# Parameter loads re-spaced, the tail's gap in another buffer, and more products in one pair: top-k attention with a low-rank mixer

## The chip, the cores and the metric

One core of one Trainium2 chip. The metric is the device time of the whole program in microseconds, the median of several executions. TensorE is called PE, VectorE DVE, ScalarE ACT, GpSimd POOL and SyncE SP.

## The reference

```python
# q, k, v: (8, 8, 576, 64);  top_k = 32
scores = q @ k.transpose(0, 1, 3, 2) / sqrt(64)
kth = np.partition(scores, -32, axis=-1)[..., -32:-31]
scores = np.where(scores >= kth, scores, -1e9)
attn = np.exp(scores - scores.max(-1, keepdims=True))
attn = attn / (attn.sum(-1, keepdims=True) + 1e-9)
x = (attn @ v).transpose(0, 2, 1, 3).reshape(8, 576, 512)
# U: (576, 32), V: (32, 576), w_ch1: (512, 2048), w_ch2: (2048, 512)
u = x + (x.transpose(0, 2, 1) @ U @ V).transpose(0, 2, 1)
out = u + np.maximum(u @ w_ch1, 0) @ w_ch2
```

The four mixer parameters arrive as 64-bit floats and are turned into 32-bit floats on the chip.

## The kernel before

**Work.** A "pair" is two heads of one batch; there are 32 pairs, four to a batch. The 576 query rows of a pair are cut into four tiles of 128 and a tail of 64. In the first batch each of the five tiles is a step of its own (steps n = 0 to 19, `ALONE` = 20). From the second batch on a pair has four steps, and the last of them holds tile 3 and the tail together, so step 23 is the first joint tail step. A step of the loop works on several tiles at once: scores for step n+1, the top-k search for step n, transposes, values and mixing for earlier steps.

**Top-k** runs on DVE: eight maxima at a time (L521, L539), which are then replaced by a large negative number (L534). In later pairs the row is first folded into an `upper` and a `lower` half: L395 copies the scores, L446 and L449 (POOL) and L448 (DVE) fold, L500 and L502 search the lower half. L448 of step n+1 stands inside the search of step n. `front` is a generator that writes this out in stages. For a tail in a joint step, the search works on a copy in a one-buffer tile `tplace` (slot 2 of the lanes).

**Gaps.** After the search, scores below the 32nd are pushed down: ACT forms a `gap` from the score and the threshold `least` (L565, L568), POOL subtracts it (L569), and ACT takes the exponential (L453). The gap lies in the tile `E`, a ring of two buffers. In a joint tail step there are three gaps.

**Queues.** Each engine runs its instructions in the order in which the loop writes them. On ACT the copy of a values product, `XT<-O` (L717), frees a buffer of the PSUM ring `tp` that the transposes (L631) need. From pair 6 on the transposes of whole tiles go by DVE (L595) and by DRAM (`away`, then `PT<-away`).

**Parameters.** They come in 36 parts: U in two, V in two, then 16 of `w_ch1` and 16 of `w_ch2`. `next_params(k)` makes one stage of a pipeline: it joins the parts whose passes are done, starts the passes of those that have been loaded, and issues k loads on SP. A part costs a load into `raw` (three buffers), three ACT passes (L179, L180, L183), one DVE shift (L202, or L193 for the last eight), and two POOL additions (L203, L205). The passes are put out one at each call of `fill`, the rest at the next `next_params`.

**Products.** The MLP of a batch is written as a generator that gives one matmul at a time: L842 for the first layer, L859 for the second, over 320 and then 256 rows. `fill`, called eight times a step, deals them out by a debt: each call adds `part` to `due`, and products are issued until `due` is paid. With no product left, `due` is set to 0. `part` is `share`, with a factor 1.4 in a joint tail step, and with a factor under 1 during the second batch:

```python
if n <= ALONE + BATCH + 2:
    part *= SECOND if ALONE + NT <= n < ALONE + 2 * NT else EARLY
```

The last batch's MLP (`closing`, L935) is computed after the attention in a Strassen-like form.

Of the kernel before, what the change touches and what calls it, by code (L numbers as in the profile page):

```python
# [8 lines left out]
F32 = mybir.dt.float32  # L9
# [17 lines left out]
def kernel(  # L27
# [29 lines left out]
    B, H, S, D = q.shape  # L57
    P = 128
# [4 lines left out]
    NT, TAIL = 4, 64  # L63
# [3 lines left out]
    NPAIR = H // 2  # L67
# [3 lines left out]
    ALONE = NPAIR * CH  # L71
# [11 lines left out]
    attn = ctx.enter_context(tc.tile_pool(name="attn", bufs=2))  # L83
# [63 lines left out]
    def f64_raw(srcs):  # L147


        n, w = srcs[0].shape[0], srcs[0].shape[-1]  # L150
        raw = mlpp.tile([P, 2 * C], U32, tag="raw", name="raw", bufs=3)
        if len(srcs[0].shape) == 3:
            raw = raw.rearrange("p (f w) -> p f w", w=w)
        else:
            raw = raw[:, 0:w]
        for i, src in enumerate(srcs):
            nc.sync.dma_start(raw[i * n : (i + 1) * n], src)
        return raw[0 : len(srcs) * n]

    def f64_parts(raw, out):  # L160

        n, w = raw.shape[0], raw.shape[-1] // 2
        d = "p f" if len(raw.shape) == 3 else "p"
        low, hi = (raw.rearrange(f"{d} (w two) -> {d} w two", two=2)[..., i] for i in range(2))
        low8 = raw.bitcast(U8).rearrange(f"{d} (w eight) -> {d} w eight", eight=8)[..., 3]
        if out is None:
            if not spare:  # L170

                uT = mlpp.tile([P, NC, S], F32, tag="uT", name="uT")
                words = uT.rearrange("p c n -> p (c n)").bitcast(U32)
                spare.extend(words[:, i * SLAB : (i + 1) * SLAB] for i in range(NT))
            out = spare.pop()[0:n, 0:w]
        bits = out.bitcast(U32)
        lows, his = low.bitcast(F32), hi.bitcast(F32)
        passes.extend((
            lambda: nc.scalar.activation(bits.bitcast(F32), his, AF.Copy, scale=RESCALE),  # L179
            lambda: nc.scalar.activation(  # L180
                lows, low8, AF.Identity, bias=four[0:n], scale=-(1 + 2.0**-10) * 2.0**-26
            ),
            lambda: nc.scalar.activation(his, his, AF.Sign, bias=nudge[0:n]),  # L183
        ))
        return hi, bits, low, len(params) < LATE

    def f64_join(hi, bits, low, late, outs):

        if late:
            none = nought if len(bits.shape) == 2 else nought.rearrange("p o -> p o ()")
            nc.vector.scalar_tensor_tensor(  # L193
                out=bits,
                in0=bits,
                scalar=3,
                in1=none.to_broadcast(list(bits.shape)),
                op0=ALU.logical_shift_left,
                op1=ALU.bitwise_or,
            )  # L200
        else:
            nc.vector.tensor_single_scalar(bits, bits, 3, ALU.logical_shift_left)  # L202
        nc.gpsimd.tensor_tensor(bits, bits, hi, ALU.add)  # L203
        for dst, form in outs:
            nc.gpsimd.tensor_tensor(dst.bitcast(U32), form(bits), form(low), ALU.add)  # L205
# [26 lines left out]
    def next_params(n):  # L232

        while passes:
            passes.pop(0)()
        while parts:
            f64_join(*parts.pop(0))
        while raws:
            r, outs = raws.pop(0)
            if isinstance(outs, list):  # L240
                parts.append((*f64_parts(r, None), outs))
                continue
            made = f64_parts(r, outs)
            parts.append((*made, [(made[1], same)]))
        for _ in range(min(n, len(params))):
            srcs, outs = params.pop()
            raws.append((f64_raw(srcs), outs))
# [6 lines left out]
    def load(g):  # L254

        list(loading(g))
# [177 lines left out]
    def split(g, t):  # L434

        if (g, t) in folds:
            pair(g, t, 1)

    def pair(g, t, stage):
        S2 = S2s[g, t]  # L440
        n = S2.shape[1]
        upper, lower = folds[g, t]
        top, bottom = upper[:, 0:n, 0:HALF], lower[:, 0:n].bitcast(U32)
        a, b = (ends_of(probs[g, t], i) for i in range(2))
        if stage == 0:
            nc.gpsimd.tensor_tensor(bottom, a.bitcast(U32), b.bitcast(U32), ALU.add)  # L446
        else:
            nc.vector.tensor_tensor(top, fronts_of.pop((g, t)), b, ALU.max)  # L448
            nc.gpsimd.tensor_tensor(bottom, bottom, top.bitcast(U32), ALU.subtract)  # L449
# [18 lines left out]
    def front(tiles):  # L468
# [5 lines left out]
        for g, t in tiles:  # L474
# [4 lines left out]
            n = S2.shape[1]  # L479
# [61 lines left out]
        for c, chunk, total, _, way in lanes:  # L541
            if way == "pooled":
                gap = attn.tile([P, S], F32, tag="E", name="E")
# [17 lines left out]
        if gaps:  # L561
            slots = [lane[0] for lane in gaps]
            lo, hi = min(slots), max(slots) + 1
            least = small.tile([P, 3], F32, tag="least", name="least", bufs=3)
            nc.scalar.mul(least[:, lo:hi], m8[:, lo:hi, 7], WIDEN)  # L565
            for c, chunk, *_ in gaps:
                gap = attn.tile([P, S], F32, tag="E", name="E")
                nc.scalar.activation(gap, chunk, AF.Relu, bias=least[:, c : c + 1], scale=-WIDEN)  # L568
                nc.gpsimd.tensor_tensor(chunk, chunk, gap, ALU.subtract)  # L569
            yield  # L570
# [586 lines left out]
    BATCH = NPAIR * NT  # L1157


    SLOTS, LONG, EARLY, SECOND = 8, 1.4, 0.91, 0.84  # L1160
    share = MLP_WORK / (NPAIR * SLOTS * (NT - 1 + LONG))
    fillers, mixing, due = [], [], 0.0

    def fill(k=1):


        nonlocal due
        for _ in range(k):
            if passes:
                passes.pop(0)()  # L1170
            if mixing and next(mixing[0], True):
                mixing.pop(0)
            part = share * (LONG if len(tiles(n)) > 1 else 1)
            if n <= ALONE + BATCH + 2:
                part *= SECOND if ALONE + NT <= n < ALONE + 2 * NT else EARLY
            due += part
            while due > 0:
                if not fillers:
                    due = 0.0
                    break  # L1180
                done = next(fillers[0], None)
                if done is None:
                    fillers.pop(0)
                elif not done:
                    due = 0.0
                else:
                    due -= done

    def tiles(n):

        return steps[n] if 0 <= n < STEPS else []
# [16 lines left out]
            yield from turns(g, t)  # L1208

    load(0)  # L1210
    next_params(3)
    t = 0
    for _ in prep(0):
        pass
# [3 lines left out]
    for n in range(STEPS + 2):  # L1218
        if n < STEPS:
            g, t = steps[n][0]  # L1220
            if t == 0 and g < NPAIR:
                load(g + 1)
            if t == (1 if g < NPAIR else 2) and g + 1 < NP:
                ready = prep(g + 1)
            fronts[n] = front(steps[n])
            next(fronts[n])
            if owed:
                inverse(owed.pop(), 0, 2 * NT + 1)
        else:
            t = NT  # L1230
        here, last = fronts.get(n, iter(())), fronts.pop(n - 1, iter(()))
        if n >= ALONE - 1 and n <= ALONE:
# [12 lines left out]
            if n < ALONE:  # L1245
                split(*steps[n + 1][0])
                next(here)
                next(here)
                inverse(g, 0, 2 * NT)
                mixing.append(mixed(g, 1))  # L1250
                fill()
                next(here)
                continue
            fill()
            scores(*steps[n + 1][0])
            fold(*steps[n + 1][0])
            next(here)
            while mixing:
                fill()
# [64 lines left out]
        if n < STEPS and n - 2 >= ALONE and len(tiles(n - 2)) > 1:  # L1324
            scale(steps[n - 2][0][0])
        next(here, None)
        if g == NPAIR and t < NT - 1:
            next_params(1)
        fill()
        if n >= STEPS:  # L1330
# [4 lines left out]
        next(here, None)  # L1335
        for tile_ in tiles(n + 1):
            split(*tile_)
        fill()
        next(here, None)
        for tile_ in tiles(n - 1):  # L1340
# [9 lines left out]
                coming = loading(g + 2) if g + 2 < NP else iter(())  # L1350
            next(coming, None)
        next(ready, None)
        if t != 0 or g == NPAIR + 1:
            next_params(1)
        next(here, None)
        fill()
# [36 lines left out]
```

## Time and profile before

| what | value |
|---|---|
| median of 3 runs | 1660.74 us (1660.58 to 1660.79) |
| profiled execution | 1660.23 us, its span 1658.0 us |
| mean granted PE clock | 0.968 |
| PE busy | 1555.6 us (94%) |
| DVE busy | 1546.9 us (93%) |
| ACT busy | 992.0 us (60%) |
| POOL busy | 1009.4 us (61%) |

Steps 0 to 19 end at about 202 us, the second batch's first pair (steps 20 to 23) at about 253 us, and the attention's last search at 1509 us. The PE records give a matmul as two records, one for each pass. A "gap" is idle time of an engine before an instruction, and the releaser is what ended it. Idle time of an engine off the critical path costs nothing by itself.

### The profile page before, as it was taken

What the parts mean: (1) busy time and instruction counts of PE and PEld (TensorE: products, weight loads), DVE (VectorE), ACT (ScalarE), POOL (GpSimd) and SP (SyncE); (2) the same over time, 40 slices, a digit from 0 to 9 for tenths busy, and PEclk for the clock granted to TensorE, in tenths of its full rate; (3) what the DMA queues carried; (4) which work ended last, traced back from release to release, by engine and by line L of the source; (5) the groups of instructions that cost most, each with busy time, mean ns of one, the idle gap of its engine ahead of it and who ended that gap; (6) DMA issues with size and microseconds to landing.
All of it is one profiled execution on the core that took longest, in us unless ns stands there. A gap on an engine that the chain in (4) does not pass through costs nothing.

```text
span 1658.0 us, 30248 instructions
## 1 busy us (share of the span) xinstructions
PE 1555.6 (94%) x9638; PEld 1182.7 (71%) x9638; DVE 1546.9 (93%) x4394; ACT 992.0 (60%) x2475; POOL 1009.4 (61%) x881
## 2 busy tenths in 40 slices
PE   4566698999999999999999999999999999999999
PEld 2344466787677877788777877788777877787776
DVE  7999998999999999999999999999999999994452
ACT  5888886665655566566655656565655656564320
POOL 4888756666656565656656565656666565653620
PEclk7787799999999999999999999999999999999999
DMA  4333321254445555454545455454545455543001
GB/s 113 98 101 99 86 76 25 57 133 135 126 130 137 133 154 133 131 139 130 134 125 141 128 154 133 134 137 131 133 126 141 128 151 134 136 123 109 7 2 28
DMA packets 280399, 189.42 MB, mean 114 GB/s; under 512 B 174288, under 2 KB 261168, under 8 KB 280240
## 3 DMA queue, kind: packets, MB, share of 16 engines
q1 hardware_dynamic: 259728, 117.62, 29.4%
q10 hardware_dynamic: 20512, 69.87, 13.1%
q8 instruction: 76, 1.25, 0.3%
q14 instruction: 83, 0.68, 0.1%
HBM read 116.49 MB, written 70.91 MB: 113 GB/s over the span
## 4 chain that ended last, share of the span: by engine, by line
PE 74%; DVE 19%; DMA 2%; POOL 1%; ACT 1%; issue 1%; SPq 1%; ACTq 0%; DVEq 0%; POOLq 0%
PE mm L859 23%; PE mm L842 22%; PE sc L350 7%; DVE m L539 7%; PE O L708 6%; DVE upper L534 6%; PE mm L935 3%; DVE first L521 2%; PE sc L382 2%; PE sc L935 2%; PE tp L935 2%; PE up L782 2%; PE O L705 1%; PE tp L631 1%; DMA PT<-away 1%
## 5 line engine op out<-in xcount | busy, mean ns | idle before, releaser
L842 PE MATMUL mm<-uT,w 128*128 128x320 f32 (+1 forms) x1792 | 463.3, 410 | 2.2 <-POOL uT L798 2.2
L859 PE MATMUL mm<-hT,w 128*128 128x320 f32 (+1 forms) x1792 | 460.2, 407 | 0.0
L569 POOL TENSOR_TENSOR Ssb<-Ssb,E 128x576 f32<-128x576 f32 x243 | 339.7, 1418 | 187.0 <-ACT E L568 187.0
L842 PEld LDWEIGHTS mm<-uT,w 128*128 128x128 f32 x1792 | 334.6, 191 | 102.0 <-issue 7.4
L859 PEld LDWEIGHTS mm<-hT,w 128*128 128x128 f32 x1792 | 332.0, 190 | 92.6 <-issue 10.2
L539 DVE MAX8 m<-upper 128x8 f32<-128x304 f32 (+1 forms) x774 | 362.3, 508 | 0.7
L534 DVE MATCH_REPLACE8 upper<-m,upper 128x304 f32<-128x304 f32 (+1 forms) x516 | 256.5, 504 | 0.0
L449 POOL TENSOR_TENSOR lower<-lower,upper 128x576 uint32<-128x576 uint32 x108 | 152.3, 1410 | 135.9 <-DVE upper L448 133.7
L446 POOL TENSOR_TENSOR lower<-Ssb 128x576 uint32<-128x576 uint32 x108 | 152.3, 1410 | 133.4 <-ACT Ssb L395 73.5
L453 ACT ACTIVATE Ssb<-Ssb,nmax 128x576 f32<-128x576 f32 x258 | 201.8, 784 | 15.7 <-POOL Ssb L545 7.8
L350 PE MATMUL sc<-qkT 64*128 64x288 f32 (+1 forms) x1056 | 177.2, 457 | 13.9 <-ACT Ssb L404 12.2
L568 ACT ACTIVATE E<-Ssb,least 128x576 f32<-128x576 f32 x243 | 176.2, 769 | 4.2
L502 DVE MAX8 upper<-lower 128x8 f32<-128x288 f32 x432 | 171.7, 438 | 2.7 <-POOL lower L449 2.7
L395 ACT COPY Ssb<-sc 128x576 f32<-128x576 f32 x216 | 127.6, 644 | 68.3 <-PE sc L350 68.1
L595 DVE STREAM_TRANSPOSE y<-Ssb 128x512 f32<-128x512 f32 (+1 forms) x312 | 154.0, 543 | 1.2 <-ACT Ssb L453 1.2
L708 PE MATMUL O<-PT,va 128*64 128x128 f32 x2048 | 143.7, 284 | 0.0
L854 ACT ACTIVATE hT<-mm 128x320 f32<-128x320 f32 (+1 forms) x224 | 91.2, 407 | 81.7 <-PE mm L842 78.7
L350 PEld LDWEIGHTS sc<-qkT 64*128 64x128 f32 (+1 forms) x1056 | 94.8, 195 | 54.7 <-issue 16.5
L708 PEld LDWEIGHTS O<-PT,va 128*64 128x64 f32 x2048 | 112.2, 139 | 16.2 <-issue 1.6
L534 DVE MATCH_REPLACE8 upper<-first,upper 128x304 f32<-128x304 f32 x216 | 97.4, 458 | 0.0
L500 DVE MATCH_REPLACE8 lower<-upper,lower 128x288 f32<-128x288 f32 x216 | 93.9, 442 | 0.0
L717 ACT COPY XT<-O 128x128 f32<-128x128 f32 x128 | 33.8, 264 | 98.3 <-PE O L708 94.0
(268 smaller groups left out, 2259.7 us busy)
## 6 DMA issues: line engine op xcount, KB each, us to landing
away<-y SPq DMA_DIRECT2D x416, 144.0 KB
PT<-away ACTq DMA_DIRECT2D x104, 576.0 KB
raw<-in_moe_w_ch_dram SPq DMA_DIRECT2D x32, 512.0 KB
va<-in_v_dram SPq DMA_DIRECT2D x64, 128.0 KB
scale<-rd ACTq DMA_DIRECT2D x56, 144.0 KB
out_dram<-ob SPq DMA_DIRECT2D x59, 128.0 KB
ld<-in_q_dram SPq DMA_DIRECT2D x108, 64.0 KB
ld<-in_k_dram SPq DMA_DIRECT2D x108, 64.0 KB
```

The costliest lines, as they stand in the source:

```text
L350: nc.tensor.matmul(out, lhsT=qkT[half(h), 0, cols(t)], rhs=qkT[half(h), 1, lo:hi], start=True, stop=True,)
L446: nc.gpsimd.tensor_tensor(bottom, a.bitcast(U32), b.bitcast(U32), ALU.add)
L453: nc.scalar.activation(E, chunk, AF.Exp, bias=nmax, scale=SCALE, accum_out=total)
L502: nc.vector.max(spot, lower)
L534: nc.vector.match_replace(nxt, ms[c], curs[c], NEG)
L539: nc.vector.max(ms[c], curs[c])
L568: nc.scalar.activation(gap, chunk, AF.Relu, bias=least[:, c : c + 1], scale=-WIDEN)
L569: nc.gpsimd.tensor_tensor(chunk, chunk, gap, ALU.subtract)
L595: nc.vector.transpose(y[:, :, i * NT : i * NT + c].rearrange("p r c j -> p c r j"), E2[:, a : a + c * P].rearrange("p (c r j) -> p c r j", ...
L708: nc.tensor.matmul(O[half(h)], lhsT=va[:, h, j, :], rhs=PT[:, NT * h + j], start=False, stop=(j == NT - 1),)
L842: nc.tensor.matmul(phs[f][:, 0:w], lhsT=first_layer(cc, f), rhs=uT[:, cc, lo:hi], start=(cc == 0), stop=(cc == NC - 1),)
L859: nc.tensor.matmul(po[:, 0:w], lhsT=w2[:, f, c * P : (c + 1) * P], rhs=hTs[f][:, 0:w], start=(f == 0), stop=(f == NF - 1),)
```

## The change

Four edits. The first `next_params` asks for two loads in place of three. The calls in the steps 21 to 23 are spread differently: three in step 21, three in step 22 and one in step 23, in place of two, two, one and one more in step 24. The tail's gap (slot 2) is written into `tplace` in place of `E`. The factor on `part` becomes one for each of the second batch's pairs: 1.1, 0.82, 0.91, 0.91, where it was 0.91, 0.84, 0.91, 0.91.

```diff
             for c, chunk, *_ in gaps:
-                gap = attn.tile([P, S], F32, tag="E", name="E")
+                if c == 2:
+                    gap = attn.tile([P, S], F32, tag="tplace", name="E", bufs=1)
+                else:
+                    gap = attn.tile([P, S], F32, tag="E", name="E")
                 nc.scalar.activation(gap, chunk, AF.Relu, bias=least[:, c : c + 1], scale=-WIDEN)
                 nc.gpsimd.tensor_tensor(chunk, chunk, gap, ALU.subtract)
...
-    SLOTS, LONG, EARLY, SECOND = 8, 1.4, 0.91, 0.84
+    SLOTS, LONG, EARLY = 8, 1.4, (1.1, 0.82, 0.91, 0.91)
...
             if n <= ALONE + BATCH + 2:
-                part *= SECOND if ALONE + NT <= n < ALONE + 2 * NT else EARLY
+                part *= EARLY[min(max(n - ALONE, 0) // NT, NT - 1)]
...
     load(0)
-    next_params(3)
+    next_params(2)
...
         next(here, None)
-        if g == NPAIR and t < NT - 1:
+        if g == NPAIR:
             next_params(1)
         fill()
...
         for tile_ in tiles(n + 1):
             split(*tile_)
+        if g == NPAIR and t < NT - 1:
+            next_params(1)
         fill()
...
         next(ready, None)
-        if t != 0 or g == NPAIR + 1:
+        if g == NPAIR and t < NT - 1:
             next_params(1)
         next(here, None)
```

## The prediction

> **What bounds the kernel now.** I read the page's busy lines and its 40 slices first, then a table of stretches of 20 us, then who waited for whom between 202 and 345 us, and last the order in time on three engines around the largest stall.
>
> ```profile
> span 1658.0 us, 30248 instructions
> PE 1555.6 (94%) x9638; PEld 1182.7 (71%) x9638; DVE 1546.9 (93%) x4394; ACT 992.0 (60%) x2475; POOL 1009.4 (61%) x881
> ...
> PE   4566698999999999999999999999999999999999
> ...
> DVE  7999998999999999999999999999999999994452
> ```
>
> Two engines are full, but not over the same time. DVE is full from slice 2 on and PE from slice 7 on; PE's share before that cannot be filled with MLP products, since these need the first batch's `uT`, and L842 first runs at 212.4 us.
>
> ```profile
> 240.00:260.00 20.00, 12.75 (x70) 9.04 (x69) 19.54 (x50) 9.36 (x22) 12.44 (x10) 0.89 0.11 17
> 260.00:280.00 20.00, 20.00 (x143) 14.99 (x143) 18.81 (x61) 14.24 (x37) 13.75 (x11) 0.94 0.16 40
> ...
> 640.00:660.00 20.00, 20.00 (x130) 14.71 (x126) 20.00 (x62) 13.27 (x34) 10.69 (x11) 1.00 0.54 143
> ```
>
> The columns are PE, PEld, DVE, ACT, POOL, granted PE clock, DMA share, GB/s. In 240 to 260 PE stands for 7.25 us and the clock is not full; from 260 on PE is dense and DVE is the one with holes; at 640 both are dense. DVE's gaps over 100 ns between 202 and 345 us add up to 7.3 us, and from there to 1495 us to under 0.5 us. So DVE paces 345 to 1500: a pair takes it 46.46 us every time (steps of 14.70, 11.40, 10.35, 10.01). At the end PE waits for the last probabilities again (1.37 us at 1517.8, 0.77 at 1528.0), so the tail hangs on DVE. What moves DVE at 330 us moves the end by as much.
>
> ```profile
> PE tp L631 <- ACT XT L717: 7.3, 1, 7.3
> ```
>
> ```profile
> DVE upper L448 <- ACT Stail L415: 3.4, 2, 2.5
> DVE upper L502 <- POOL lower L449: 1.9, 3, 1.0
> DVE y L595 <- ACT Ssb L453: 1.2, 2, 0.7
> DVE upper L448 <- ACT Ssb L395: 0.8, 1, 0.8
> ```
>
> One PE wait, and four kinds of DVE waits that sum to 7.3. The DVE waits come after it: PE is late with the scores because of it. Its cause, in order of time on ACT and then on POOL (start, length, instruction, and in brackets the idle time before it with its releaser):
>
> ```profile
> 252.65 0.21 ACT L565 ACTIVATE least<-m 128x3 f32<-128x3 f32 x1 [5.72 <-DVE m L539]
> 252.88 1.44 ACT L568 ACTIVATE E<-Ssb,least 128x576 f32<-128x576 f32 x2
> 257.32 0.78 ACT L568 ACTIVATE E<-Stail,least 128x576 f32<-128x576 f32 x1 [3.00 <-POOL Ssb L569]
> 258.00 0.74 ACT L183 ACTIVATE raw<-raw,nudge 128x512 f32<-128x512 f32 x1
> 258.65 0.42 ACT L854 ACTIVATE hT<-mm 128x320 f32<-128x320 f32 x1
> 258.96 0.26 ACT L717 COPY XT<-O 128x128 f32<-128x128 f32 x1
> ```
>
> ```profile
> 253.28 1.29 POOL L203 TENSOR_TENSOR w<-w,raw 128x512 uint32<-128x512 uint32 x1 [3.28 <-DVE w L193]
> 254.65 1.28 POOL L205 TENSOR_TENSOR w<-w,raw 128x512 uint32<-128x512 uint32 x1
> 255.88 2.77 POOL L569 TENSOR_TENSOR Ssb<-Ssb,E 128x576 f32<-128x576 f32 x2
> ```
>
> In step 23 the tail's gap is the third `E` of a ring of two. It waits for POOL's first subtraction, which stands behind a parameter's join. Behind the tail's gap on ACT stand a parameter pass, an `hT` and the `XT` copy that frees the buffer PE needs.
>
> **The change, part by part.** Step numbers are the loop's n; which instruction stands where is read from the two programs' order.
>
> *Parameters.* All 36 shifts (L202, L193) remain. Up to the start of step 20 there are 28 instead of 29: DVE and the MLP's start gain the 0.67 us of the L193 at 194.5. Steps 20 to 23 hold eight before the tail step's last maxima instead of five. The eight L193 rows run 0.64 to 1.44 us, mean 0.91; the long ones begin while a POOL subtraction or product runs and end about 0.55 us after it. Three more cost 2.7 us at the mean (1.9 to 4.3 at the ends). The last maxima, over at 252.61 before, end at 252.61 - 0.67 + 2.7 = 254.6. Given back behind them: the shifts at 252.54 (0.67) and 262.66 (1.16).
>
> On a page: the Trainium skill, "SBUF — State Buffer" ("two separate sides"), calls the port pair of VectorE and GpSimd "an exclusive lock, not a bandwidth split", the loser waiting for a whole instruction. This speaks against three joins in a step: if each of the three added shifts met the start of a subtraction of 1.4 us, they would cost 6.1 us, and the sum below would end near 0.8 us. The rows agree with the rule (1.33 and 1.44 us where POOL was busy, 0.64 to 0.67 where it was idle), but 0.70 us between two subtractions that follow each other shows that not every meeting costs a whole one.
>
> Queues passed: V's main load (four DMAs on SP) goes behind the second pair's eleven; these end at 17.7 us, so it lands by about 22 at the 126 GB/s of that stretch. ACT stands at its first pass ahead of step 0's `least`; before, it stood 8.7 us until 25.3 for V's tail at the same place, so nothing is later. In step 20 a second parameter load stands ahead of four `ld` issues on SP and holds them from 215 to about 222, until a join frees its buffer; L320 reads them at 235.5. POOL's join in step 23 now stands ahead of k=0's L449, but L449 waits for a fold on DVE that by my count ends some 2 us after the join. All this is costed at nothing; without that cover each would cost one join, 2.65 us.
>
> *The tail's row.* The gap in `tplace` waits only for DVE's last maximum on that row, which `least` needs anyway. In step 23 this and the moved join take 3.00 us of wait, the pass (0.65 net) and one `hT` (0.31) off ACT between 252.61 and the end of `XT` at 259.23: 6.62 becomes 2.66 us, and `XT` is done at 257.3. In the other 27 tail steps ACT's wait (26.2 us in all over 28) is worth nothing: DVE is dense there and does not read what ACT is late with.
>
> *Products.* A 128x320 product is two records of 0.27 us, 0.54 us of PE. In program order seven more are dealt by the values that run at 234.9 us before and ten by those at 247.8 (5.4 us); nine are still ahead at 288 (4.85), eight at 312 (4.3), eleven of the 256-wide ones (0.43 us each, 4.75) from 348 to 403, and none from 425 on. The batch's products only run out earlier, at 403 to 425 us, where PE waits for probabilities anyway (1.75 us at 403.1, 2.2 at 431.5). So the end has not one product less; what this part does is to fill the hole.
>
> PE reaches the transposes behind the hole at 252.03 - 0.67 + 5.39 - 0.54 (one product now stands after them) - 0.85 (two short gaps that close) = 255.4, and goes on at 257.3 with `XT` instead of 259.28: 2.0 us sooner, 0.54 of it returned by that one product. The granted clock was 0.50 from 255.5 to 262.3, in which PE worked 3.0 us; at full clock that is 1.5 us less. A gap of 1.75 us at 403 left the clock at 1.00, one of 2.2 us at 431 came with 0.91; the remaining 1.9 lies between, so this term is 0 or 1.5, and I take 1.5. By 323 us 1.2 us of products are paid back. Sum for PE at the scores of 326 us: 2.0 - 0.5 + 1.5 + 1.2 = 4.2 us sooner.
>
> The page "TensorE: Matmul & The Clock Gate" (Part 1) says that the clock halves after an idle window of about 3.4 us. By it 1.9 us would be safe and the sum 4.2; by the row of 2.2 us with its 0.91, which speaks against that rule, the sum would be 2.7.
>
> DVE: -0.67 + 2.7 - 0.67 - 1.16 = +0.2 at 263.7; then the waits for scores go, 0.80 and 2.52, giving -3.1. The 1.04 at 286.4 stays, since `oT` (0.87) now stands ahead of that L449 on POOL. The waits of 0.36, 0.67, 0.54 and 0.49 go, two of them because `oT` moves behind L449: -5.2, more than PE has, so the scores at 328.7 come with PE's -4.2. **Forecast: 4.2 us less.** The profiled execution took 1660.23 (span 1658.0 and 2.2 around it), 0.5 under the median of 1660.74; the difference goes on the median: 1656.5.
>
> **Rivals.**
> *The hole still halves the clock* (1.5 us lost), or the longer idle at 403 to 425 does it there. Each window of 3.4 us at half costs PE 1.7; behind 430 us its scores come as little as 0.4 us ahead of DVE. For: the 0.91. Against: PE gains about 1 us on DVE at 425. Either gives about 1658.0, within the 0.2%.
>
> *DVE pays more for its shifts.* At 1.44 us for each of the three, with the others dearer too, the maxima end at about 258 and the gain shrinks to 0.7: 1660.0. For: POOL has three joins of 2.65 and 2.8 us of subtractions in steps of 11 us. Against: it idled 3.3 to 3.6 us in each of these steps.
>
> *Slower: the ring of three raw buffers.* A load's turn is 4.0 us from issue to first pass at least (a row with no ACT wait), 2.15 of passes, 0.9 shift, 2.65 join: 9.7 us for three, against DVE steps of 11 to 12 us. If the landing took 10 us, a turn would be 15.7, DVE would stand some 4 us in both steps and end about 8 later: 1664.5. It decides from a landing of about 6 us; no row shows one.
>
> *The edits do nothing here* (every gain met by another wait in 260 to 330): 1660.7.
>
> **How the numbers follow.** A measurement tells 0.2%, 3.3 us, from no change. Forecast 0.55 (below 1657.4); clock or dearer shifts 0.29 and no effect 0.08 give 0.37 for the same; the ring 0.08. Lower bound: all 7.3 us of DVE's waits gone, 1653.4, so 1653.5; upper: dear shifts, 1660.0.
>
> **What would show it.** Right: no PE gap over 2.5 us near 255 us and a granted clock of 1.00 up to 280; ACT's tail gap without a wait; DVE's gaps in 255 to 345 under 3.5 us; eight L193 in steps 20 to 23 of 7 to 8 us; MLP products gone some 5 us earlier near 420. Wrong: ACT waiting at L179, DVE waiting at L193, or DVE's end moving by less than its step at 330.

## Result and the profile after

The changed kernel takes 1663.53 us (median of 22 runs, 1660.35 to 1665.85) against 1660.47 (22 runs, 1659.14 to 1661.83) of the kernel before: ratio 1.0016 with a 95% interval of 1.0009 to 1.0022, 3.1 us the other way from the forecast of 4.2 us less. A second set of 11 runs gave 1662.04 and 1.0011 (1.0002 to 1.0019). The profiled execution took 1661.79, with a span of 1659.6; it lies 1.7 us under the median, so the lines from it show about half of the loss. The changed kernel has three more lines above the tail's gap: what was L568 is L571 there, L631 is L634, L717 is L720, L842 is L845 and L854 is L857.

First, who waited for whom on the vector engine between 202 and 345 us (us in total, times, longest):

```profile
DVE w L193 <- ACT w L179: 3.2, 2, 1.7
DVE upper L502 <- POOL lower L449: 1.9, 1, 1.9
DVE upper L448 <- PE mm L862: 1.5, 1, 1.5
DVE upper L448 <- ACT Stail L415: 1.5, 1, 1.5
DVE y L598 <- ACT Ssb L453: 0.2, 1, 0.2
```

The lower four stand where the 7.3 us of before stood; 5.1 us are left there. The first is new and stands ahead of them: DVE waits at a parameter's shift for the first of that parameter's three passes on ACT.

PE in the same stretch, and the table of stretches (columns as in the prediction):

```profile
PE tp L634 <- ACT XT L720: 2.9, 1, 2.9
PE tp L639 <- ACT PT L635: 1.9, 1, 1.9
```

```profile
240.00:260.00 20.00, 17.99 (x108) 12.67 (x106) 20.00 (x42) 11.36 (x28) 11.81 (x10) 1.00 0.15 25
260.00:280.00 20.00, 18.98 (x117) 13.72 (x118) 19.96 (x69) 14.99 (x38) 14.79 (x11) 0.91 0.18 40
400.00:420.00 20.00, 16.76 (x129) 13.78 (x129) 19.97 (x65) 10.49 (x28) 13.17 (x11) 0.91 0.64 165
420.00:440.00 20.00, 16.53 (x91) 10.62 (x88) 20.00 (x60) 11.74 (x30) 11.54 (x12) 1.00 0.44 125
```

The hole of 7.25 us shrank to 2.93, but it ends at 260.92 us where it ended at 259.28, and the clock still loses a stretch of half speed behind it (0.91 of 20 us; the clock is 0.50 from 261.5 to 264.8 us, half as long as in the kernel before). The copy that PE waits for, in order of time on ACT:

```profile
258.38 0.21 ACT L565 ACTIVATE least<-m 128x3 f32<-128x3 f32 x1 [4.53 <-DVE m L539]
258.61 1.44 ACT L571 ACTIVATE E<-Ssb,least 128x576 f32<-128x576 f32 x2
259.96 0.76 ACT L571 ACTIVATE E<-Stail,least 128x576 f32<-128x576 f32 x1
260.63 0.24 ACT L720 COPY XT<-O 128x128 f32<-128x128 f32 x1
```

No wait stands between the subtraction's gap and the tail's any more, and from the last maxima to the end of `XT` it is 2.5 us instead of 6.6. But ACT starts at 258.38 instead of 252.65: DVE's last maxima end 5.7 us later. These 5.7 us more than undo the 4.1 us saved behind them. They add up as -0.7 of an earlier start, +3.2 of the two waits, and +3.25 of shifts (eight L193 sum to 8.03 us, five to 4.78).

Now the first wait on both engines. DVE and then ACT, in order of time:

```profile
219.25 1.40 DVE L539 MAX8 m<-upper 128x8 f32<-128x576 f32 x2
222.14 1.58 DVE L193 SCALAR_TENSOR_TENSOR w<-w,nought 128x512 uint32<-128x512 uint32 x1 [1.49 <-ACT w L179]
```

```profile
215.81 0.98 ACT L857 ACTIVATE hT<-mm 128x320 f32<-128x320 f32 x2 [1.48 <-PE mm L845]
...
220.13 0.44 ACT L857 ACTIVATE hT<-mm 128x320 f32<-128x320 f32 x1
220.58 0.78 ACT L453 ACTIVATE Ssb<-Ssb,nmax 128x576 f32<-128x576 f32 x1
221.26 0.18 ACT L453 ACTIVATION_READ_ACCUMULATOR Ssb<-Ssb,nmax 128x1 f32 x1
221.36 0.19 ACT L525 ACTIVATE nmax<-first 128x2 f32<-128x2 f32 x1
221.45 0.66 ACT L179 ACTIVATE w<-raw 128x512 f32<-128x512 f32 x1
```

ACT waits for nothing at L179: the raw words are there. The pass is simply late in ACT's own order, behind exponentials and evictions of products. A call to `next_params` deals the passes of the words that have come, and the next call deals their shift. In the kernel before, two rounds of maxima lie between these two calls, and the same pass and its shift, on ACT and on DVE, run without a wait:

```profile
221.61 0.66 ACT L179 ACTIVATE w<-raw 128x512 f32<-128x512 f32 x1
```

```profile
224.67 0.67 DVE L193 SCALAR_TENSOR_TENSOR w<-w,nought 128x512 uint32<-128x512 uint32 x1
```

The pass is no later in the changed kernel (221.45 us). With the third call only one round lies between, and it is DVE that comes earlier.

### The profile page after: what moved, and what is told of

Its sections match the earlier page's. It is cut to its first block, busy times and chain, and to the rows that moved or that the text cites. A ratio compares the mean times of both kernels' runs of the same rounds, so it can differ in the third digit from the quotient of the medians.

```text
span 1659.6 us, 30243 instructions
## 1 busy us (share of the span) xinstructions
PE 1557.6 (94%) x9638; PEld 1183.1 (71%) x9638; DVE 1547.6 (93%) x4394; ACT 991.8 (60%) x2475; POOL 1009.4 (61%) x881
## 4 chain that ended last, share of the span: by engine, by line
PE 72%; DVE 20%; DMA 3%; ACT 2%; issue 1%; SPq 1%; POOL 1%; DVEq 0%; ACTq 0%; POOLq 0%
PE mm L862 23%; PE mm L845 21%; PE sc L350 7%; DVE m L539 6%; PE O L711 6%; DVE upper L534 6%; PE mm L938 3%; DVE first L521 2%; PE tp L938 2%; PE sc L938 2%; PE sc L382 2%; PE up L785 2%; PE O L708 1%; DVE y L598 1%; PE tp L634 1%
## 5 line engine op out<-in xcount | busy, mean ns | idle before, releaser
L845 PE MATMUL mm<-uT,w 128*128 128x320 f32 (+1 forms) x1792 | 462.8, 409 | 2.6 <-POOL uT L801 2.3
L845 PEld LDWEIGHTS mm<-uT,w 128*128 128x128 f32 x1792 | 333.7, 190 | 104.3 <-issue 11.5
L539 DVE MAX8 m<-upper 128x8 f32<-128x304 f32 (+1 forms) x774 | 362.3, 508 | 0.7
L571 ACT ACTIVATE E<-Ssb,least 128x576 f32<-128x576 f32 x243 | 176.2, 768 | 4.2
L857 ACT ACTIVATE hT<-mm 128x320 f32<-128x320 f32 (+1 forms) x224 | 91.5, 409 | 86.4 <-PE mm L845 81.9
L720 ACT COPY XT<-O 128x128 f32<-128x128 f32 x128 | 34.0, 266 | 114.8 <-PE O L711 110.1
```

The source lines that it names most:

```text
L539: nc.vector.max(ms[c], curs[c])
L845: nc.tensor.matmul(phs[f][:, 0:w], lhsT=first_layer(cc, f), rhs=uT[:, cc, lo:hi], start=(cc == 0), stop=(cc == NC - 1),)
```

## Experiments

Theory A: the calls amid two steps cost what the other two parts gain, by these waits. Rivals: the products cost (D), or the gains are met by other waits (B). All times are medians; the difference is taken to the kernel before of the same set of runs.

| kernel | parts | us | difference | last maxima end | `XT` done | hole of PE near 260 | DVE's scores (L448) at about 328 |
|---|---|---|---|---|---|---|---|
| before | none | 1660.47 | 0 | 252.61 | 259.23 | 7.25 | 328.7 |
| e1 | tail | 1657.67 | -3.40 | 252.66 | 256.17 | 4.14 | 326.0 |
| e2 | parameters | 1663.41 | +2.34 | 256.84 | 260.66 | 5.21 | 330.1 |
| e3 | products | 1659.96 | -1.11 | 251.76 | 258.06 | 2.20 | 327.6 |
| e4 | tail, parameters | 1663.10 | +2.53 | 257.25 | 260.10 | 4.23 | 329.8 |
| e5, e11 | tail, products | 1654.77, 1655.41 | -5.80, -5.96 | 253.84, 251.40 | 257.03, 254.59 | none | 325.6, 323.1 |
| e6 | parameters, products | 1665.07 | +4.50 | 258.62 | 262.12 | 3.92 | 331.6 |
| after, e7 | all | 1663.53, 1662.04 | +3.06, +0.97 | 258.34, 258.82 | 260.87, 261.35 | 2.93, 2.95 | 330.4, 332.1 |

The columns from the fifth on are of one profiled execution each, whose own time lies up to 2.4 us from the median of its row (e5 above it; e2, e4, e6 and after 1.6 to 2.1 below). e5 and e11 have five runs each.

**e1, the tail's row alone.** The first hunk of the change.

> The kernel before with the tail's gap in the tail's row, and nothing else of the change. Theory A (the change loses by two waits of the vector engine for a parameter's pass, 1.49 and 1.72 us, that the products and the third call make together; each part by itself does what it was costed at): ACT's tail gap starts at about 254.3 instead of 257.3 us, the transposed copy that frees PE's buffer ends at about 256.2 instead of 259.2, PE's hole of 7.25 us shrinks to about 4.2, the clock still halves, and the time falls by 2 to 3 us, to 1657.5 to 1658.7. Theory B (what the scores gain is met by other waits behind 260 us): 1660.5, within 0.5 us of before.

1657.67 us, ratio 0.998 (0.9971 to 0.9989): theory A, and B falls. ACT in order of time:

```profile
252.70 0.21 ACT L565 ACTIVATE least<-m 128x3 f32<-128x3 f32 x1 [5.72 <-DVE m L539]
252.94 1.44 ACT L571 ACTIVATE E<-Ssb,least 128x576 f32<-128x576 f32 x2
254.28 0.76 ACT L571 ACTIVATE E<-Stail,least 128x576 f32<-128x576 f32 x1
...
255.92 0.24 ACT L720 COPY XT<-O 128x128 f32<-128x128 f32 x1
```

The tail's gap starts at 254.28 and the copy ends at 256.17. The hole is 4.14 us, and DVE's scores come 2.7 us sooner.

**e2, the parameter calls alone.**

```
-    next_params(3)
+    next_params(2)
...
-        if g == NPAIR and t < NT - 1:
+        if g == NPAIR:
             next_params(1)
...
+        if g == NPAIR and t < NT - 1:
+            next_params(1)
...
-        if t != 0 or g == NPAIR + 1:
+        if g == NPAIR and t < NT - 1:
             next_params(1)
```

> The kernel before with the parameter calls of the change, and nothing else of it. Theory A: without the added products ACT is not held by evictions of products, so the vector engine stands under 1 us in all ahead of the eight L193; these cost the 2.7 us of three more; the join no longer stands ahead of step 23's subtraction, so the copy that frees PE's buffer ends within 1 us of the 259.2 of before; 1659.5 to 1661.5. Theory C (one fill between two calls is enough for the wait, products or not): waits of 1.5 us and more at two of the eight, the last maxima at about 258 us, PE's hole over 9 us, and 1663 or more.

1663.41, ratio 1.0015 (1.0006 to 1.0024). Theory A falls and C has the time right: the waits at L193 are 2.6 us without a single added product (1.70 at 222.0 and 0.90 at 235.0). The three calls are enough for the waits. C's sizes were too large: only one wait is over 1.5 us, the last maxima end at 256.8 instead of about 258, and the hole is 5.21 us, not over 9.

**e3, the products alone.**

```
-    SLOTS, LONG, EARLY, SECOND = 8, 1.4, 0.91, 0.84
+    SLOTS, LONG, EARLY = 8, 1.4, (1.1, 0.82, 0.91, 0.91)
```

> The kernel before with the change's dealing of products, and nothing else of it. Theory A: PE's hole of 7.25 us near 255 is filled down to about 2 us and the clock does not halve there, or only after it; no wait at L193, since the shift stands two fills behind its pass; nothing is gained but the clock's 1.5 us: 1659 to 1660.7. Theory D (the products are what costs: ACT waits for them, and later holes of over 2 us near 415 and 432 us halve the clock): 1662 or more, with a granted clock of about 0.9 in 400 to 440.

1659.96, ratio 0.9991 (0.9982 to 1.0). The hole is 2.20 us and the mean clock in 240 to 260 us 0.96 instead of 0.89; behind the hole it is still 0.50, but from 258.2 to 261.6 us only. No wait at L193. Theory A, and D falls as the main cause. The gain of 1.1 us is not clear of the noise: the interval reaches 1.0, and the runs spread over 5.5 us (1657.06 to 1662.59).

**e7, the changed kernel again.**

> The changed kernel itself, once more beside the others. Median 1663 to 1664, with runs spread from 1660.4 to 1665.9 as before. If the spread comes of a few microseconds of idle PE that halve the clock in one run and not in another, a profile of over 1663 has more stretches with a granted clock under 1.00 than the one of 1661.8, and the same order of instructions; if it comes of landings of transfers, it has other waits for a DMA.

1662.04, under the median that was expected, spread 1660.76 to 1666.35. Its profile was of a run of 1663.68, 1.9 us over the first. Of that, 0.5 us is there at the last maxima (the two waits at L193 are 4.2 us here, and the first shift is 0.8 us shorter). The other 1.2 are there when DVE gets the scores after the hole (285.6 us instead of 283.9); the granted clock in 260 to 280 us is 0.83 instead of 0.91, one more stretch of half speed. No DVE wait for a DMA is behind it. So a half-clock stretch goes with most of what parts these two runs; that such stretches make the whole spread was not shown.

**e5 and e11, tail's row and products, without the parameter calls** (two sets of runs of one kernel).

> The kernel before with the tail's row and the products, without the parameter calls. Theory A (the parameter calls are what costs): no wait at L193; the copy that frees PE's buffer ends at about 256.2 us and PE reaches it at about 256.9, so the hole is under 1 us and the clock stays full there; the time is at or under that of the tail's row alone, 1655 to 1657.7. Theory D (the added products cost, by holes of over 2 us from 400 to 435 us that halve the clock, and they do so in some runs and not in others): median 1658 to 1660.5 with a spread of 4 us or more, against the 2 us of the tail's row alone.

> The tail's row and the products once more, beside the others: 1654.5 to 1655.5, the fastest of all, 5.5 to 6.5 us under before. Its first profile was of its slowest run (1657.14 us), with a clock of 0.66 in 180 to 202 us; if the early clock is what parts its runs, a profile of a run near 1654.8 has a higher clock there and ends its last maxima 1 to 2 us sooner, at 252 to 253 us, with the same order behind.

1654.77 and 1655.41, ratios 0.9968 (0.9955 to 0.998) and 0.9963 (0.9951 to 0.9976): the fastest of all, under both kernels of the change. All that is left of DVE's waits in e11, and the stretch where the hole was:

```profile
DVE upper L448 <- ACT Stail L415: 1.5, 1, 1.5
DVE upper L502 <- POOL lower L449: 1.0, 1, 1.0
DVE y L598 <- ACT Ssb L453: 0.2, 1, 0.2
```

```profile
240.00:260.00 20.00, 20.00 (x106) 14.29 (x103) 20.00 (x52) 15.50 (x36) 12.46 (x10) 1.00 0.09 14
260.00:280.00 20.00, 19.90 (x151) 14.82 (x150) 19.96 (x64) 14.20 (x37) 16.19 (x15) 1.00 0.17 40
```

PE and DVE are both full from 240 to 260 us at full clock: what the prediction wanted from the three parts, two of them do. e5's profile was of its slowest run, with a clock of 0.66 in 180 to 202 us; e11's had 0.84 there and ended its last maxima 2.4 us sooner, a little more than expected. One expectation failed: e5's profile has a wait of 0.8 us at L193, at 224.74 us, without the parameter calls. e11's has none, so DVE can come to that shift a little ahead of ACT's pass in the old spacing too; the calls make it two waits of 2.3 to 4.4 us in all.

**e4 and e6, the parameter calls with one other part.**

> The kernel before with the tail's row and the parameter calls, without the products. Theory A: the two waits at L193 are those of the parameter calls alone, 2.5 to 2.8 us, the hole of PE near 260 us is about 4 to 5 us, and the time is the tail's 1657.7 and the 2.3 us of the calls together, 1659.5 to 1661. Theory E (the calls already undo what the tail's row gains, since the vector engine and not the gap is then what the copy waits for): 1661.5 to 1663.5, no better than the calls alone.

> The kernel before with the parameter calls and the products, without the tail's row. Theory A: two waits at L193 of 3 us or more in all, since two products' evictions that wait for PE now stand ahead of the pass on ACT in step 20; the tail's gap waits about 1.4 us for a subtraction again; PE's hole near 260 us is 4 to 5 us; 1663 to 1665, above the change with all three parts. Theory D (products alone decide): within 1 us of the change.

e4: 1663.10, ratio 1.0014 (1.0005 to 1.0023), theory E: with the calls, the tail's row gains nothing over e2. The subtraction that the tail's gap waited for is no longer behind a join there, so there is only about 1 us to save (3.8 us from maxima to `XT` in e2, 2.85 in e4). e6: 1665.07, ratio 1.0026 (1.0016 to 1.0035), theory A, with 4.4 us of waits at L193: two products' evictions stand ahead of the pass and wait for PE, as in the lines of after at 215.81. So the parts are not a sum. The calls cost 2.3 us alone, 5.9 over the tail's row, 6.8 to 9.0 over tail's row and products.

**e8, the change with the passes dealt earlier.** The passes of the words that have come are dealt ahead of the step's exponentials; shifts and joins stay. Its lines behind the edit are four further on than in the changed kernel (L539 is L543, L571 is L575). The edit, shortened and with remarks added:

```
+        if g == NPAIR and t < NT - 1:
+            parted()              # the loop over raws, out of next_params
         fill()
...
-            next_params(1)
+            next_params(1, 1 if t < NT - 1 else 0)   # joins all but one
```

> The changed kernel, with the three passes of a parameter dealt one call earlier in steps 20 to 22 of the loop, ahead of the step's exponentials on ACT; the joins, shifts and loads stay at their places and every other engine keeps its order. Theory A (the vector engine's waits at L193 are waits for L179, which stands on ACT behind two exponentials and an eviction of a product): L179 ends at about 220 and 234.5 us, the two waits (3.2 to 4.2 us) are under 0.4 us in all, the tail step's last maxima end about 3 us sooner, at 255, and the time falls by 2 to 3.5 us against the changed kernel, to 1659 to 1660.5. Theory C2 (something else holds the vector engine there, the load of the raw words or the join on POOL): the waits stay at 3 us with another releaser, and the time stays within 1 us of the changed kernel's.

1660.41, ratio to before 1.0 (0.9991 to 1.0009): 0.2 us under its own before, where the change was 1.0 and 3.1 over. No wait at L193 is left; yet the last maxima end at 258.08, as late as ever. That was not expected of either theory. DVE, then POOL, in order of time:

```profile
219.56 1.40 DVE L543 MAX8 m<-upper 128x8 f32<-128x576 f32 x2
220.89 1.79 DVE L193 SCALAR_TENSOR_TENSOR w<-w,nought 128x512 uint32<-128x512 uint32 x1
...
225.38 1.63 DVE L193 SCALAR_TENSOR_TENSOR w<-w,nought 128x512 uint32<-128x512 uint32 x1
```

```profile
218.08 2.79 POOL L576 TENSOR_TENSOR Ssb<-Ssb,E 128x576 f32<-128x576 f32 x2 [3.36 <-ACT E L575]
220.82 1.30 POOL L203 TENSOR_TENSOR w<-w,raw 128x512 uint32<-128x512 uint32 x1
222.20 1.62 POOL L205 TENSOR_TENSOR w<-w,raw 128x512 uint32<-128x512 uint32 x1
...
225.16 1.29 POOL L205 TENSOR_TENSOR w<-w,raw 128x512 uint32<-128x512 uint32 x1
```

The shift that no longer waits starts while POOL adds, and ends 0.55 us after POOL's instruction: 1.79 and 1.63 us, where 0.67 would do. Three of the eight begin inside an addition of a join like that (1.79, 1.63 and 1.73 us) and three more inside another instruction of POOL, and the eight sum to 10.82 us. The wait did not go away; it moved into the shift. What e8 gains it gains behind the maxima: PE's hole there is 0.43 us, and the clock in 260 to 280 us is 1.00.

**e9, two loads at first instead of three, over tail's row and products.** It was meant to give the load saved to the end of step 20 as well, but that step is written out on a branch of its own which the edited line does not reach: the trace has five shifts before the last maxima as before, and one more at 271.6 us. So it tests the change's "two at once at first" alone.

```
-    next_params(3)
+    next_params(2)
...
-        if t != 0 or g == NPAIR + 1:
+        if g in (NPAIR, NPAIR + 1):
             next_params(1)
```

> The tail's row and the products, with two loads instead of three at once at first, and the load so saved given to the end of step 20, so that no step of 20 to 22 has more than two joins. Theory F (it is the third join in a step that costs: the shift meets ACT's late pass or a busy POOL there; what the second pays is the 0.7 us of the rows): the last maxima end 0.67 us sooner by the start and 0.7 to 1.5 later by the added shift, within 1 us of the tail's row and products alone, 1654 to 1655.8, and no wait at L193 over 1 us. Theory G (each join dealt into steps 20 to 22 costs 1.9 us, whichever it is, as the 5.7 us of three did): 1656 to 1657.5.

1655.94, ratio 0.9968 (0.9956 to 0.998), 5.4 us under before: within 0.5 us of tail's row and products. The start costs and gains nothing beyond that, so the loss of the change is the calls in steps 21 to 23, of which three each stand in 21 and 22. Neither F nor G was tried.

**e10, e8 with four joins left out on POOL**, those of the first and second calls in steps 21 and 22. The calls that choose them are not shown.

```
             nc.vector.tensor_single_scalar(bits, bits, 3, ALU.logical_shift_left)
+        if not join:
+            return
         nc.gpsimd.tensor_tensor(bits, bits, hi, ALU.add)
```

> The kernel with the passes dealt early, with POOL's two additions left out of four joins, those of the first and second calls of the first two steps after 214 us, so that these parameters come out wrong; DVE's eight shifts, ACT's passes and the loads stay. Theory H (with the waits gone, the shifts run 1.53 to 1.79 us each because POOL works at the same time: the price of a third join is paid on the vector engine as a wait or as a longer shift): the shifts that begin after a subtraction fall to about 0.7 us, the one at 231 that begins inside one stays at 1.4 to 1.6, the eight sum to 7.5 to 8.5 us instead of 10.8, the last maxima end at 255 to 256 instead of 258.1, and the time falls by 1 to 3 us, to 1657.5 to 1659.5. Theory I (the shifts are long for what they read and write, not for POOL): the eight still sum to over 10 us and the time stays at 1660 to 1661.

1657.25, ratio 0.9976 (0.9968 to 0.9985), theory H, a little beyond its ranges. DVE in order of time:

```profile
220.33 1.02 DVE L193 SCALAR_TENSOR_TENSOR w<-w,nought 128x512 uint32<-128x512 uint32 x1 [0.62 <-ACT w L179]
...
224.44 0.69 DVE L193 SCALAR_TENSOR_TENSOR w<-w,nought 128x512 uint32<-128x512 uint32 x1 [0.31 <-ACT w L179]
```

The two shifts of 1.79 and 1.63 us run 1.02 and 0.69 (the first still meets the end of a subtraction), and the third that met an addition runs 0.67 instead of 1.73; the one that begins inside a subtraction still runs 1.24. The eight sum to 7.24 us instead of 10.82. Of these 3.6 us, 2.8 are the three that met an addition; 0.8 is the first shift, at 206 us, ahead of the joins that are left out. Waits for L179 of 0.9 us come back, since DVE is early again. The last maxima end at 255.10, `XT` at 257.63, and 3.2 us of time go (4.0 when each is taken against the kernel before of its own set). The instruction on DVE is the same; what changed is how long POOL is busy beside it.

## Why the prediction was wrong

**The step that failed** is the costing at nothing of what the parameter calls move: "All this is costed at nothing; without that cover each would cost one join". It followed the calls past SP's queue and POOL's, and past ACT's at step 0 alone. In steps 21 and 22 it did not ask where on ACT the pass stands that the shift reads. It named the sign (DVE waiting at L193) but priced it only as a slow landing, which "decides from a landing of about 6 us". The landing was short: in the change a load issued at 223.20 us let its pass start at 226.95, 3.75 us later, and that was the one pass that waited for a transfer, 1.0 us, with no DVE wait behind it. The wait came from the distance of two calls, 3.2 us that no term held. The ring rival's 1664.5 us is the figure of the prediction that is nearest to 1663.53, but by luck: its landing of 10 us did not come.

**The shifts' term** was mis-sized as well, a little: three more at the "mean 0.91" are 2.7 us, and they took 3.25 in this profile and 2.5 in e7's (7.30 us for the eight), where the waits are 4.2. The two errors put the last maxima at 258.3 instead of 254.6 us. The rival of dearer shifts had that place right ("about 258"), by the other of the two causes, and e8 shows that they replace each other. But it let 0.7 us of gain stand, and by its own figures none could: 258 and the 2.66 us from there put `XT` at 260.7, 1.4 us later than before.

**On the port**, the prediction counted against the rule a row that fits it. The Trainium skill, "SBUF — State Buffer" ("two separate sides"), describes the ports that VectorE and GpSimd share as a lock that one of them holds for a whole instruction, for VectorE when it reads two inputs from SBUF and GpSimd reads there too. The prediction set its 6.1 us for three whole meetings aside for one row of 0.70 us. But that shift began at 229.36 us, 0.15 us before the first of two subtractions on POOL ended, and ended 0.55 us after it; the second subtraction, which began inside the shift, ran 1.87 us instead of 1.41. In all thirteen profiles every L193 that begins inside an instruction of POOL ends 0.54 to 0.55 us after that one, so a meeting costs what is left of it. For the change itself the mean of the rows was the nearer figure even so: 3.25 and 2.5 us against 2.7. Only in e8, without the waits, the eight shifts cost 10.82 - 4.78 = 6.0 us more than the five of before, and that this is near 6.1 is partly luck, since the meetings were not those that the 6.1 counted. In the change waits and shifts together cost 6.5.

**The tail's row** was right: 6.62 us "becomes 2.66", measured 2.5 in the change and 3.5 alone. Alone it is worth 3.4 us.

**The products** were right in kind: they filled the hole (7.25 to 2.20 alone, none with the tail's row), at a gain of 1.1 us alone (not clear of the noise) and 2.4 to 2.6 with the tail's row. But PE was to reach the transposes at 255.4 us and reached them at 258.0: 1.89 us of it is a new hole at 233 us, where PE waits for ACT's copies to `PT`. It goes with the calls: every kernel that has them shows it (1.75 to 2.57 us, and 0.30 in e10 without the joins), the others do not.

**The clock.** The hole was to be 1.9 us and was 2.93, and the clock halved. The rule of about 3.4 us on the page "TensorE: Matmul & The Clock Gate" (Part 1) would have kept it full there; it did not hold in these rows. Nor does the prediction's own reading, by which the clock halves from some length between 1.75 and 2.2 us on, hold in all runs (last section).

**The end** was right: the time follows DVE's step at about 328 us. Time less that start is 1331.3 to 1331.7 us in eleven of the thirteen profiled executions (1332.8 in e8, 1333.5 in e3). With the parameter calls left out the reasoning comes out near e5 and e11, which took 1654.8 and 1655.4: an estimate with e1's `XT` at 256.17, 3.1 us sooner than before, gives 3.1 - 0.5 + 1.5 + 1.2 = 5.3 us less in place of 4.2, or 1655.4.

## What to carry to other kernels

When a change deals work closer together, ask for each instruction that is moved up on the full engine where its producer stands in the producer's own order, not only whether its data has landed: the pipeline over three engines had a smallest distance between its calls here. Taking such a wait away gains nothing on that engine if the instruction then starts inside another engine's and pays the same time in its own length: price the wait and the meeting together. Here undoing the placement gained more than undoing the wait. Parts of a change are not a sum: two that gain 3.4 and 1.1 us one by one gain 5.9 together, and the third, which costs 2.3 alone, costs 6.8 to 9.0 on top of them.

## What the hardware showed that was not expected

- A shift of 0.67 us on DVE ran up to 1.79 us beside POOL's additions, and POOL's addition that began inside it ran 1.62 instead of 1.29 (e8, lines above): both sides pay, and the shift ended 0.55 us after the addition that it met.
- An idle stretch of PE does not by its length alone decide the half clock. In the change 2.28 us at 414.9 came with a clock of 0.91 in its 20 us and 2.25 at 433.1 with 1.00; in the kernel before 2.21 at 431.4 came with 0.91; in e1 2.27 at 400.6 and 2.25 at 428.7 both came with 1.00. The widest pair: in e10 3.34 us that ended at 411.0 left the clock of 400 to 420 us at 1.00, while in e5 1.66 us that ended at 420.4 were followed by 0.50 from 421.5 to 428.3. What else decides it stays open, and so does why the runs of the change and of e3 spread over 5.5 us and those of e1 over 2.1.
